# Two stacked attention layers on one core: the last 128-row TensorE products rewritten as pairs of 64-row products, with a new order table

## The chip, the cores and the metric

The kernel runs on one NeuronCore of a Trainium2 chip. The metric is the device time of one execution in microseconds (us), from start to end; lower is better. A core has TensorE (PE, matrix products into PSUM), VectorE (DVE), ScalarE (ACT), GpSimd (POOL) and SyncE (SP, which here issues DMAs and nothing else). Each engine works through its own queue in order; semaphores tie the queues together. PSUM has 128 partitions and eight banks of 512 f32 values each.

## The reference, cut to what matters

The input x is 2048 tokens of 512 bf16 values. Two layers of A and B follow each other, each with a layer norm in front and a residual behind, 32 heads of 16 dimensions:

```python
x = x + A(layernorm(x)); x = x + B(layernorm(x))     # twice
# A: 4 segments of 512 tokens; causal softmax attention within a segment,
#    mixed by a gate per head with a linear-attention memory of earlier segments
a_dot = softmax(q @ k.T * scale + mask) @ v
a_mem = (phi(q) @ M) / (phi(q) @ z + 1e-6)            # M, z summed over earlier segments
o = g * a_mem + (1 - g) * a_dot;  return o @ wo
# B: linear attention over all tokens with a learned feature map per head
phi_q = concat(softmax(q @ w_phi), softmax(-(q @ w_phi)))     # phi_k alike
o = (phi_q @ (phi_k.T @ v)) / (phi_q @ sum(phi_k) + 1e-6);  return o @ wo
```

## The kernel before, in words

Sixteen token tiles of 128 rows stay in SBUF as X. The program first describes the whole computation as a list of 2729 operations (class Graph), each with its reads and writes, the engines that could do it and a modelled duration. The order of the work is not computed in the kernel: a packed table, ORDER (L1181), holds for every operation its place in one global order and its engine, and for every tile its buffer. `place` (L157) unpacks it, and `emit` (L190) gives each engine its operations in that order with the semaphore waits that the dependencies need. Tile pools are small: PSUM is pool pD, four tiles of two banks each, so a product can only start when an earlier tile's copy out of PSUM is done.

The helpers matter for reading the profile, because a line there is the helper's:

- `mm` (products at L326) and `pair` (products at L341). Nearly all products contract over 64 rows: the lower and the upper half of the array work on two products at the same time, which write two different banks. `pair` makes one projection out of two operations: in the first, the halves of the array work on one half of the contraction of each of two outputs, in the second they swap. The second waits for the first (`hard`). In the table they are separate operations (labels such as KQ and KQ2), so other work can stand between them.
- `evac` (ScalarE copy at L359, VectorE copy at L360): a copy out of PSUM, on the engine that the table names. ScalarE also does all exponentials (`act`, L351).
- `tpe` (L371, products at L378): transposes a 128 x 512 block as four 128-row, 128-column products against the identity, into bf16 values in one bank, followed by one `evac`. It is used for the blocks listed in PE_T (L1171): the first four normalised tiles of layer 0 and of layer 1 (xnT, xA), tile 15 of the second norm in each layer (xnT, xB), one attention output in each layer (otr), and the four transposed key features of the first segment (PhKtr). All other transposes are DMA transposes (L364).
- `fold_weights` (L548): multiplies the transposed B query and key weights by the block-diagonal w_phi, eight operations of four 128-row, 128-column products each (label fold, seen at L326), each with an `evac` into WB.
- `o_T` (L885, products at L894): for six tiles of B's output (blocks ("b", ...) in PE_T) the sum of the two halves and the transpose are done at once, with eight 128-row, 128-column products, two accumulated into each of four column blocks of one bank (label otp), followed by an `evac` (ote).
- `setup` (L450) loads, makes constants and computes the gates from one small product (label beta); `warm` (L652) issues 26 products of 512 columns over 128 rows at the start, with some smaller ones in the middle, whose result nobody uses.

Per layer, `build` (L1106) goes over four segments: norm, projections (`a_proj`), attention for two tiles at a time (`a_att`), output projection, second norm, B's keys (`b_keys`); then over four chunks of B's queries (`b_query`), with the next layer's norm and projections behind each chunk. In the span, the first layer's attention lies roughly from 10 to 185 us, its B queries from 207 to 232, the second layer's attention from there to 400, and its B queries from 427 to the end.

Of the kernel before, what the change touches and what calls it, by code (L numbers as in the profile page):

```python
# [12 lines left out]
BF16 = mybir.dt.bfloat16  # L13
# [284 lines left out]
class Kernel:  # L298
# [72 lines left out]
    def tpe(self, out_ap, src, reads, writes, opens=(), label="", ev=None):  # L371

        ps = self.T(self.pD, "gen")
        pb = lambda: ps.t[:, :].bitcast(BF16)[:, 0:512]

        def fn(e):
            for k in range(4):
                ins = e.transpose(pb()[:, k * 128:(k + 1) * 128], src()[:, k * 128:(k + 1) * 128], self.ident[:])  # L378
# [71 lines left out]
    def setup(self):  # L450
# [74 lines left out]
        self.mm(lambda: [(pb.t[:, 0:H], self.onesb[:], self.beta_sb[:], True, True)], [H], [R("beta0"), R("onesb")], [pb], label="beta")  # L525
# [22 lines left out]
    def fold_weights(self):  # L548
# [12 lines left out]
        for k in ("k", "q"):  # L561
# [90 lines left out]
    def warm(self):  # L652
# [232 lines left out]
    def o_T(self, key, o, ores, pair=None):  # L885
        R = self.R
        oT = self.oT[key] = self.T(self.p1, "oT")
        if pair is not None:
            tp = self.T(self.pD, "gen")

            def fn(e):
                for k in range(4):
                    for sgn in range(2):
                        ins = e.matmul(tp.t[:, k * 128:(k + 1) * 128], pair.t[:, (k // 2) * 512 + sgn * 256 + (k % 2) * 128:(k // 2) * 512 + sgn * 256 + (k % 2) * 128 + 128],  # L894
                                       self.ident[:], start=sgn == 0, stop=sgn == 1)
# [290 lines left out]
6=sjk_%$N<cBVm5bf)gMs4uYRyBILp0m=8PR2pkL>Aun!%UtlHt3I%X8`~(HD6TXHx*cAt3TpWtsa0m{=__zcU;8L6e_wg;Q0^;cq52wLuNQjwWCd`F?)SpITYwUre
unl&`HP9Wq;94k*MQ|Q0!=Eq@FwTcJ@Dsg-p7;%{z;9s;F2~}y74G2A)C*T)MI4PqaW{;`arllhLkWz)N>~ib;sh**kr;(p;2ms%iC7X#VR@{8Ww0`?!zwrfOJh~6h
HG#=&cwB-a0))a=lC=Jg4MAG{)z&(!3$i48mHoFG?)nYLI5Pj{ZI(U<1y$%ed#zHftvUk&cQ<v1CK%=9)^eb3&lc*ckv#6hY}y5X2YN31o{Fe;aseR6KOJzq1spnU*
k*s0Fe*|vEVU|rCB%|=ixM*j~lQ!jic$f5C_l#EJ5RGASI_sG?`M+_xJ<G#JU(8>!HOjF&G=;SD2CtQxVES2OuY9rEHXo4nl6qPMRz;zo#Y`fP(9z;|ACef2F4Qftq
0s`bf=j1sSrGhgMPqe2wp+5w^f6$V+dq2L<6<+(h{(1bb2_zQc{Uj2vyI<+KTrHe*RDMFprR?ZaY}pO(;4+K)+S5EZ0CREA1ZQaXTx=@5ov818}{7{FU_CrS>aZ}0<  # L1190
_rE)ZchEfu&OG&XFeT!Rh7w*Pnv<J&meQH1{Fd1$`qG6O0dr@N=PO0!U9Y&xXz_b$%;(H9BCRCY5(<tgqRj4-Ap^;RTYEm^CK^18cHKayViKb8uszudlF*T)T)SMLW
#qF4iDiClB5_ALu`3<F}sdNgb(R7+cGw3wVq`0((&fr=)hw*4G&896hhrXe8^bvz7Ic|seG>_&}OIlB>Xf=IFt!O-dMHBcK_T}T)kAvx3+Dai5N=GpvoyXSHhEC!M{
ET+c7qo%4(bu$#cG7m*NSClb58%s~hxgKG{+#yEZpzDJIEqr^S&X0y7)~)Lj4t98yo&p1KeeS!6iKPMCy(Vc+>3)a7YFk=PC&UiEgzr|K1i`)0mY<H?o12mG!)@TF2
qH-Fh_AQF3vZxH{ZfO9D~F7HkRg6oP%?60se|h@-_ULhw^nS!J9cB=jVbvjKet*C8itLj@nZf>OiNUBXy;2REA?wS&mI7Au})LEu4jy@IX$-gLxvS=RrJ#NAOf0$-{
XPPvfkdjbm~w&cNBZ9CxR<kdfoS2`JB!GI1PIbcnv-FZnRl;v*EnN2xZ?=IK0&XYge1&Q*90PvNTEgDY`mp2hWeA<yI_T%Q;5M&86p`52w1*gThy(+N65XK5avq+~p
w&(V2`!^^n>U!)aWksEMBuEUq8E?4IoT#XxZBd*DpDLG$&xZH%Bax+fJ7onPn$5*Mk*v>mRJ}2O<oPoA+MyevxP$o*mX{oA6M_1??rKjt3gPQXNTEM618{Wgac_lC9
Z+R6j;}*P@*KtcOBwBH6Zo?fp1s4{(cr|a}oxFxW@_NoEKIbChGX{}g6csn=J%8X^q=gZCxh=Qj_S}j0@qX^iUAQaXq1%+0t+-20NTI|%`i_D{ka)|NK!^arB2c{JA
1E^=<jatX4{$f`z!d}u6bHGN2oa&8qUbFuiOS*-e@}<`2%qAk{4*C5zi@F;O1$P;qO|yxYl{n9N7NM;`4Ye3AE|&SBhJ8CXdudphN6ZjD6Vi#@sLW0M^sYu6aB?$KE
r4E7$4{R^nfn&ISvz#=?T>r%|v-oPeh4wqPd76Vv1Pe1x1KR@sdt(BhgsAqN^NVBoI$2v4|()ir6BdNFtJoXVgk06LCZ$@tm%4Ymr=}5G_PXkxHZ%H~Ad&5$EAN$Ao
ZklGBJ=JV;#Umf{BY6@$ePF;v{<JA9YhiT2_icMu&#9x+mk5M4xC@g4ubc|{ZPJ+~3*L|c(wWE0s%29ZPL6uCr3@grvvnMD>+MRpQZWe?F=^c3AhS1~|z7ms+L7%qm  # L1200
1$9z?c5~IZ!F;-NQ_xT||;OcUmXex4xtl}v@;cH^Nm?0*J>*9uZ#xuopo+u`XSz@x7BBqMjVvblOR*S{rCBNWlVy>7c=8FYlp;#i8iC4T!>=tW84Y^b-7eDcIu}AC^
8^wCDNvsen#VWB`Y!IJ`FT{SaPOKH5i!a63;w!O5d?RYgL!yQ{EG~+gs+K$=YRm27Td_lI6_><8u~!@r$HY;wQydp3#5QqKoDpZm8F@~e78k@RabDC?m&FxPTip@2#
Vv7D+!go4cj9~TgZNR@k<Y~oaaNv__r-bnKs*xlWL;TbHjqu^W6@AvkQe1^aY;6k55-IIN<0xy#ZRKKY$~6LX7Y`=EUTyw;;OtNugUAOyKF8$iWah}>LYu|x1z7SA@
9haMN0{?r|czBz7zfAd(mJ1B7T%NWi>^zy1FIrOP1|r2l=bGErX<zccqpc<vkfJg_P1rD??<cjFfR@n2eIW<p5bv)mL>?UDZlHmOse`>O0w5elHuUC-P@GP=?DvGKP
#P+sJq_zDyt^q>}+Mmi$4+mI-Ai8Am3PiDjT{rQXOSvXL4rTdTLSze*}I$|5qE9H3ImOfs{4D%;8jvWc1?8>@-(nS3bU$)+lmOevGg6!N{CCYz~WWKr2!wv$~X>8=v
=blFW7ldMq}myx=JjMB~3QMFfPk&omD`CLwtljRIKQyx=O<gYTVEGhS?{i?mnDi5d*DqO#iyH$jKDTSUYU(3?6lpG~z$suyI94hyy7E0=Da*P}+hsoh`oXjb6$r19E
Y^id{f-+Qx=|Zxw?5MKK*>a>DFHfpds=N9qd#Il3v^t}Xs}l+os^t2JI;hU6v&!j1>aa?yQ|JJ_QhrdYWIFv(<(8dPFLhqEQ5RGmnMSUbb7X#9Kr200Y8_ASm#Osu8
# [70 lines left out]
```

## Time and profile before

| what | value |
|---|---|
| time, median of three runs | 469.15 us (468.43, 469.15, 469.81) |
| span of the profiled execution | 465.9 us |
| time of the profiled execution itself | not shown; the median is 3.25 us over the span |
| mean granted TensorE clock | 0.999 |

The span runs from the first to the last instruction. In the page and in the answers of the trace, a group row gives line, engine, operation, tiles, shapes and count, then the busy time in us and the mean of one in ns, then the idle time of the engine just before the group. A row of the chain gives start, length, engine, tile, line and count, following back from the last instruction whatever released each step. A row of the timeline gives start, length, engine, line and count; a length over several instructions runs from the first start to the last end, and a product's length includes the time that its result takes to come out, so products overlap and their starts tell the pace. PEld is the weight load that belongs to each product. A row of the waits gives who waited for whom, us in total, times and the longest.

### The profile page before, as it was taken

The numbers are of one execution on the slowest core, as the hardware profiler recorded it, in microseconds if no ns is written. First come the engines' busy times: TensorE is split into PE (matmuls) and PEld (weight loads), VectorE is DVE, ScalarE is ACT, GpSimd is POOL, SyncE is SP. The second block draws the span as 40 slices with busy tenths as digits, with TensorE's granted clock in tenths as the row PEclk, the third lists the DMA queues.
The fourth block names the chain that finished last, engine by engine and source line by source line (L and its number), as shares of the span: only waits on it lengthen the run. The fifth ranks groups of instructions, "written<-read, shape, count | busy, mean of one in ns | idle before, by whom it ended". The sixth has DMA issues, their size and how long they took to land.

```text
span 465.9 us, 25071 instructions
## 1 busy us (share of the span) xinstructions
PE 448.2 (96%) x11591; PEld 296.7 (64%) x11591; DVE 418.9 (90%) x801; ACT 424.3 (91%) x550; POOL 53.3 (11%) x139
## 2 busy tenths in 40 slices
PE   9999999999999999999999999999999999999886
PEld 4467656767767676655556777676677677666553
DVE  6999999999879988988999999999999787998991
ACT  4899999999999998589999999999999999686984
POOL 1401131001101101100320041010020020110000
PEclk9999999999999999999999999999999999999999
DMA  8363673403743031000143443441206104100247
GB/s 258 80 150 77 94 147 65 75 13 53 95 83 50 4 56 37 14 3 14 31 87 61 72 82 61 73 87 33 25 16 106 26 16 61 38 13 3 48 82 216
DMA packets 89386, 30.34 MB, mean 65 GB/s; under 512 B 75954, under 2 KB 89282, under 8 KB 89282
## 3 DMA queue, kind: packets, MB, share of 16 engines
q1 hardware_dynamic: 88450, 28.20, 32.5%
q8 instruction: 91, 1.49, 1.3%
q10 hardware_dynamic: 800, 0.52, 0.4%
q14 instruction: 13, 0.11, 0.1%
q0 software_dynamic: 32, 0.02, 0.0%
HBM read 6.31 MB, written 2.10 MB: 18 GB/s over the span
## 4 chain that ended last, share of the span: by engine, by line
PE 67%; ACT 26%; DVE 4%; issue 2%; POOL 1%; DVEq 0%
PE D L341 42%; PE D L326 23%; ACT p L351 12%; ACT pF L351 8%; ACT pE L351 4%; PE D L662 2%; DVE p L1091 1%; ACT pS L351 1%; PE D L378 1%; DVE p L360 1%; ACT X L359 1%; POOL rstd L590 1%; ACT p L359 0%; DVE p L601 0%; DVE p L1097 0%
## 5 line engine op out<-in xcount | busy, mean ns | idle before, releaser
L351 ACT ACTIVATE p<-D 128x1024 bf16<-128x1024 f32 (+1 forms) x224 | 222.0, 1026 | 13.2 <-PE D L341 10.0
L351 ACT ACTIVATE pF<-D 128x896 bf16<-128x896 f32 x128 | 116.1, 934 | 3.1 <-PE D L326 2.2
L326 PE MATMUL D<-pK,pQ 64*128 64x256 bf16 (+3 forms) x1536 | 114.8, 243 | 4.2 <-ACT pF L351 1.0
L326 PEld LDWEIGHTS D<-pK,pQ 64*128 64x128 bf16 x1536 | 55.1, 94 | 40.8 <-ACT pF L351 6.5
L326 PE MATMUL D<-pV,pF 64*128 64x34 bf16 x1024 | 76.4, 176 | 0.5 <-ACT pE L351 0.5
L326 PE MATMUL D<-pW,pF 64*128 64x34 bf16 x1024 | 74.1, 176 | 0.0
L326 PEld LDWEIGHTS D<-pV,pF 64*128 64x128 bf16 x1024 | 56.7, 93 | 3.7 <-issue 0.8
L588 POOL TENSOR_SCALAR rstd<-mv 128x1 f32<-128x1 f32 x60 | 15.2, 259 | 352.9 <-DVE mv L581 352.9
L326 PE MATMUL D<-pV,p 64*128 64x34 bf16 x1024 | 53.4, 176 | 0.6 <-issue 0.4
L326 PEld LDWEIGHTS D<-pW,pF 64*128 64x128 bf16 x1024 | 53.4, 93 | 1.0
L351 ACT ACTIVATE pE<-D 128x768 bf16<-128x768 f32 x64 | 52.4, 828 | 1.3 <-PE D L326 1.0
L326 PE MATMUL D<-pW,p 64*128 64x34 bf16 x1024 | 52.4, 176 | 0.0
L326 PEld LDWEIGHTS D<-pV,p 64*128 64x128 bf16 x1024 | 47.5, 93 | 3.2 <-issue 0.5
L326 PEld LDWEIGHTS D<-pW,p 64*128 64x128 bf16 x1024 | 46.0, 93 | 1.6
L326 PE MATMUL D<-tri,two 64*128 64x128 bf16 (+1 forms) x384 | 46.1, 234 | 0.0
L326 PE MATMUL D<-pV,pE 64*128 64x34 bf16 x512 | 45.1, 175 | 0.0
L580 DVE BATCH_NORM_STATS2 stats<-X 128x6 f32<-128x512 bf16 x64 | 42.7, 682 | 1.9 <-DMA X<-in_A_x_dram 1.5
L326 PE MATMUL D<-pW,pE 64*128 64x34 bf16 x512 | 43.4, 175 | 0.0
L972 DVE TENSOR_REDUCE pS<-p 128x64 f32<-128x1024 bf16 (+1 forms) x36 | 38.8, 1089 | 1.4 <-ACT p L351 1.4
L341 PE MATMUL D<-pX,WA_q 64*128 64x512 bf16 x256 | 37.1, 377 | 0.1
L341 PE MATMUL D<-pX,WA_k 64*128 64x512 bf16 x256 | 36.9, 377 | 0.1
L590 POOL TENSOR_TENSOR rstd<-rstd,mhalf 128x1 f32<-128x1 f32 x60 | 35.1, 599 | 3.1
(130 smaller groups left out, 986.2 us busy)
## 6 DMA issues: line engine op xcount, KB each, us to landing
pW<-pV SPq DMA_DIRECT2D x16, 136.0 KB, 3.1
out_dram<-X SPq DMA_DIRECT2D x7, 256.0 KB, 3.2
X<-in_A_x_dram SPq DMA_DIRECT2D x3, 512.0 KB, 5.6
pX<-in_B_wqkv_dram SPq DMA_DIRECT2D x3, 512.0 KB, 4.7
p<-p SPq DMA_TRANSPOSE x76, 3.0
pX<-p SPq DMA_TRANSPOSE x54, 3.3
WA_k<-in_A_wk_dram SPq DMA_DIRECT2D x2, 256.0 KB, 6.7
WB_o<-in_B_wo_dram SPq DMA_DIRECT2D x8, 64.0 KB, 3.0
```

The lines of the kernel that those rows point to most:

```text
L326: ins = e.matmul(out_ap, lhsT, rhs, start=st, stop=sp, tile_position=(basep(lhsT), basep(out_ap)))
L341: ins = e.matmul(out_ap, lhsT[64 * hf:64 * hf + 64], rhs[64 * hf:64 * hf + 64], start=k == 0 and i == 0, stop=k == 1 and i == len(lists[hf ...
L351: return self.g.op({"act": (dur, lambda e: e.activation(out_ap(), in_ap(), func, scale=scale))}, reads, writes, opens, label=label)
L359: ch = {"act": (n / 1.2 + 51, lambda e: e.activation(out_ap(), in_ap(), ACT.Copy)), "dve": ((340 if fast else n / 0.96 + 65), lambda e: e. ...
L360: "dve": ((340 if fast else n / 0.96 + 65), lambda e: e.tensor_copy(out_ap(), in_ap()))}
L378: ins = e.transpose(pb()[:, k * 128:(k + 1) * 128], src()[:, k * 128:(k + 1) * 128], self.ident[:])
L580: v(lambda e: e.bn_stats(self.stats[:, t, :], self.X[:, t, :]), 602, [R("X", t)], [R("st", t)], label="bn")
L588: v(lambda e: e.tensor_scalar(rs, self.mv[:, t, 1:2], LN_EPS, None, op0=ALU.add), 170, [R("mv", t)], [R("rstd", t)], eng="pool", label="rstd")
L590: v(lambda e: e.tensor_tensor(rs, rs, self.mhalf[:], ALU.pow), 540, [R("rstd", t), R("mhalf")], [R("rstd", t)], eng="pool", label="rstd")
L662: ins = e.matmul(D.t[c0:, r0 * 8:r0 * 8 + n], r[:, c0:], ones(r, n), start=True, stop=True, tile_position=(r0, c0))
L972: fn = lambda e, sgn=sgn, eo=eo, Z=Z, n=n: e.tensor_reduce(Z.t[:, 0:64 * n].rearrange("p (k s h) -> p k s h", k=n, s=2)[:, :, sgn, :], eo( ...
L1091: v(lambda e, Ns=Ns, Tm=Tm, w=w, shape=shape: e.tensor_tensor(shape(Tm.t[:]), shape(Ns.t[:]), w(), ALU.mult), 600, [Ns, AB[0], AB[1]], [Tm ...
```

## The change

Every product that used 128 rows now uses 64: a transpose, a fold and an output transpose are split over the two halves of the array, and the two halves write two different banks, each 64 columns of every block (the small gate product uses the lower half alone). So a transpose has eight products with 64 moving columns in place of four with 128, an output transpose sixteen in place of eight, and the copies out of PSUM read f32 from two banks, with the halves put side by side again by the access pattern. The transposes are ordinary products now (result f32) where they were `transpose` instructions with a bf16 result. A warm-up unit becomes two concurrent 64-row products, and the one group of small 128-row products in it is left out, so there is one operation fewer. The order table is replaced as a whole.

```diff
--- before.py
+++ after.py
@@ -371,17 +371,20 @@
     def tpe(self, out_ap, src, reads, writes, opens=(), label="", ev=None):
 
         ps = self.T(self.pD, "gen")
-        pb = lambda: ps.t[:, :].bitcast(BF16)[:, 0:512]
 
         def fn(e):
             for k in range(4):
-                ins = e.transpose(pb()[:, k * 128:(k + 1) * 128], src()[:, k * 128:(k + 1) * 128], self.ident[:])
+                for hf in range(2):
+                    r = slice(64 * hf, 64 * hf + 64)
+                    ins = e.matmul(ps.t[:, hf * 512 + k * 64:hf * 512 + k * 64 + 64], src()[r, k * 128:(k + 1) * 128], self.ident[r, r], start=True, stop=True,
+                                   tile_position=(64 * hf, 0))
             return ins
-        self.g.op({"pe": (240.0, fn)}, list(reads) + [self.R("ident")], [ps], opens=opens, label=label + "p")
+        self.g.op({"pe": (112.0, fn)}, list(reads) + [self.R("ident")], [ps], opens=opens, label=label + "p", rows=64)
+        halves = lambda: ps.t[:].rearrange("p (h x) -> p h x", h=2)[:, :, 0:256].rearrange("p h (a c) -> p h a c", a=4)
         if ev:
-            self.evac(ev[0], lambda: ev[1](pb()), 512, [ps], writes, label=label + "e")
+            self.evac(ev[0], lambda: ev[1](halves()), 512, [ps], writes, label=label + "e")
         else:
-            self.evac(out_ap, lambda: pb().rearrange("p (a b) -> p a b", a=4), 512, [ps], writes, label=label + "e", fast=True)
+            self.evac(lambda: out_ap().rearrange("p a (h c) -> p h a c", h=2), halves, 512, [ps], writes, label=label + "e")
 
     def recip(self, e, o, i):
 
@@ -522,7 +525,7 @@
         v(lambda e: e.memset(self.eps6[:], 1e-6), 70, [], [R("eps6")])
         gt = self.gt
         pb = self.T(self.pD, "gen")
-        self.mm(lambda: [(pb.t[:, 0:H], self.onesb[:], self.beta_sb[:], True, True)], [H], [R("beta0"), R("onesb")], [pb], label="beta")
+        self.mm(lambda: [(pb.t[:, 0:H], self.onesb[0:64, :], self.beta_sb[0:64, :], True, True)], [H], [R("beta0"), R("onesb")], [pb], label="beta", rows=64)
         self.act(lambda: gt[:, 0, :], lambda: pb.t[:, 0:H], ACT.Exp, 32, [pb], [R("gt")])
         v(lambda e: e.tensor_scalar(gt[:, 1, :], gt[:, 0, :], 2.0 ** 60, 1.0, op0=ALU.min, op1=ALU.add), 100, [R("gt")], [R("gt1")])
         v(lambda e: e.reciprocal(gt[:, 2, :], gt[:, 1, :]), 270, [R("gt1")], [R("gt2")])
@@ -568,10 +571,11 @@
                 self.tr(lambda W=W, dt=dt: W.t[:, :, dt * 128:(dt + 1) * 128], lambda raw=raw, dt=dt: raw.t[:, dt, :], [raw], [W[dt]], label="foldT")
             for dt in range(4):
                 ps = self.T(self.pD, "gen")
-                self.mm(lambda ps=ps, dt=dt, W=W: [(ps.t[:, g * 128:(g + 1) * 128], W.t[:, g, dt * 128:(dt + 1) * 128],
-                                                    Wbd.t[:, g * 128:(g + 1) * 128], True, True) for g in range(NG)],
-                        [128] * 4, [W[dt], Wbd], [ps], label="fold")
-                self.evac(lambda k=k, dt=dt: self.WB[k][:, dt, :], lambda ps=ps: ps.t[:, 0:512], 512, [ps], [R("WB", k, dt)], label="folde")
+                self.mm(lambda ps=ps, dt=dt, W=W: [(ps.t[:, hf * 512 + g * 64:hf * 512 + g * 64 + 64], W.t[64 * hf:64 * hf + 64, g, dt * 128:(dt + 1) * 128],
+                                                    Wbd.t[64 * hf:64 * hf + 64, g * 128 + hf * 64:g * 128 + hf * 64 + 64], True, True) for g in range(NG) for hf in range(2)],
+                        [], [W[dt], Wbd], [ps], label="fold", rows=64, dur=112.0)
+                self.evac(lambda k=k, dt=dt: self.WB[k][:, dt, :].rearrange("p (g h c) -> p h g c", g=NG, h=2),
+                          lambda ps=ps: ps.t[:].rearrange("p (h x) -> p h x", h=2)[:, :, 0:256].rearrange("p h (g c) -> p h g c", g=NG), 512, [ps], [R("WB", k, dt)], label="folde")
 
 
     def ln(self, t, xT, flex=False, pe=False, root="pool"):
@@ -663,9 +667,9 @@
                 return ins
             self.g.op({"pe": (m * max(n / 2.4 + 2.5, 26.0), fn)}, [self.R("onesb")], [D], label="warm", rows=rows if c0 == 0 else rows * 10)
         for k in range(N_WARM):
-            unit(128, 512, 1)
+            unit(64, 512, 1)
             if k == N_WARM // 2:
-                for rows, n, m in ((64, 51, 12), (64, 64, 8), (64, 256, 4), (128, 34, 8)):
+                for rows, n, m in ((64, 51, 12), (64, 64, 8), (64, 256, 4)):
                     unit(rows, n, m)
 
     def a_proj(self, L, s):
@@ -891,11 +895,15 @@
             def fn(e):
                 for k in range(4):
                     for sgn in range(2):
-                        ins = e.matmul(tp.t[:, k * 128:(k + 1) * 128], pair.t[:, (k // 2) * 512 + sgn * 256 + (k % 2) * 128:(k // 2) * 512 + sgn * 256 + (k % 2) * 128 + 128],
-                                       self.ident[:], start=sgn == 0, stop=sgn == 1)
+                        for hf in range(2):
+                            r = slice(64 * hf, 64 * hf + 64)
+                            c0 = (k // 2) * 512 + sgn * 256 + (k % 2) * 128
+                            ins = e.matmul(tp.t[:, hf * 512 + k * 64:hf * 512 + k * 64 + 64], pair.t[r, c0:c0 + 128], self.ident[r, r], start=sgn == 0, stop=sgn == 1,
+                                           tile_position=(64 * hf, 0))
                 return ins
-            self.g.op({"pe": (440.0, fn)}, [pair, R("ident")], [tp], opens=[oT], label="otp")
-            self.evac(lambda: oT.t[:], lambda: tp.t[:, 0:512], 512, [tp], [oT], label="ote")
+            self.g.op({"pe": (220.0, fn)}, [pair, R("ident")], [tp], opens=[oT], label="otp", rows=64)
+            self.evac(lambda: oT.t[:].rearrange("p (a h c) -> p h a c", a=4, h=2),
+                      lambda: tp.t[:].rearrange("p (h x) -> p h x", h=2)[:, :, 0:256].rearrange("p h (a c) -> p h a c", a=4), 512, [tp], [oT], label="ote")
         elif key in PE_T:
             self.tpe(lambda: oT.t[:].rearrange("p (a b) -> p a b", a=4), lambda: o.t, ores, [oT], [oT], label="otr")
         else:
@@ -1179,64 +1187,62 @@ ORDER = """
...
```

Unpacked against the list of operations, the two tables hold the same operations but for the warm-up group. The new one places them in another order and changes the engine of some copies: of the ten copies behind xnT transposes 6 are on ScalarE (4 before), of the six behind output transposes 2 (3 before), of the eight behind folds 1 (0 before), of the four weight permutations 1 (0 before), of 36 evacuated residuals 7 (9 before), of 18 query copies 5 (4 before); two of five memsets go from GpSimd to VectorE.

More of the change, by code (lines that the diff above doesn't have):

```diff
@@ L1186 @@
[L1186 to L1197, printed above, removed]
@@ new lines @@
+2T!OCf6AXjgFdTA1cbEtxAQ{|-QE(Z0z(@#z0r(?igI<sedSMP&0C!+C42GW}JKlwb&>M4N7!1VT&=Vd&9|(uF5Cl2!A$$&5AvLCjT(}OdKzh6ei{Lt>!BEJ6tKcc##(vNSf
+5zpo9#+FMTna6)EiQq3Fcu!cBp3tzuqCd6zOW1y!(_Mt{c%3@hqQPHr@(Vu0V^RLK86AC1++uph1edygeUL|^ued_0kYsYScH8sGiJpHI1@7A3&@7~a2V#rj0pG=hT}lUgLg
+4E4uV<m8e${jc*u_vU^W!M=g<M;;46rW9dQFZ#EtL_24Ni71YPhGm;v!{Fa|(D9D<9nE5^sZv=ipQP+WpjLGg6xM+tBTj7Gvy_yR{@CwxY&a3n^;r_dQcgQeIS=fZMahTX9n
+PJ?++2!F&kv;r&OE@145J@6|ij1_SV7DLTr@oOl88KF3q!ADpW!|@tk$3S?A-#}>`kN2=FmcX}E63gKPjKECrIX*^#Z(tjg!tyvBtKxI2f~&AHRzl?a7>S=^HLQ*+aRy4v44
@@ new lines @@
+LOnisE_wc;cTx$}o}eQI(FX_&@yv#C(8pJq=bb^#805zy(zE5Ii?#5hjNw2s06ZR93MTdd^r8%+NcLq>AzJ^zgarhLutznIE1m)fAPfFN^;V-eLiiq8c}gkB14OX29IU-GTO
+Tq8ZIoxxcv9iSfl*A6Mv(>+T^xbN3&8UkeF=+{QHsHMK6w6Ui%PKs?J>rA9P!-u_WF#4d1MOlWyqJbfN*kQUIfxtP;5bP6tk2bi6O#s$OB0jUu1sQy=;K=mjXr;9Q>UEJgWR
+!;_QnIJ*zUn<9(o4NWR?o^5rS95a>G?`X~`0!+cmlu)k-a&m#-Lzy9Q6iOTv?;Q43*1qr{i{^Oso_Pl8yu|z<Wx7qIq`||D8HtApt^Q9IIN1w{PY6<dq9)i)e%@I)=L&<r7`
+xxwP3-@$~kv~;FB6>zdlrJha5#T4b#}Vh}H~4M)SQHHY=-Fq(8%qy#5r*1JxTF9d2)^2kf^Z+Rd<^#QRn}vF07W+kPauReMnI^qdwQ-2wyXk#FHKQ`{Uz&BEfk`=4@X1I!9J
+)snmqmhy#)JE^(f7jqS=oj6o3xGqk9!#SWu+5Ad&s`>Fo^kG=;O~XdNHl4HW2e(&rBQa0{30^);U@3RYe`BFtM1@My2V8h|kCY2gs(%QOd}^ynxfh{6nqT90O4CcI+tV2L2F
@@ L1240 @@
+a)=BBaIj>hAzV|S^_q_r6eWDxIS_<Zs4zr$t%jY(VB=*h+#}L|0g(KOR{
 """
```

92 lines of the change are left out of this document (46 added, 46 removed).

## Prediction

> **What bounds the kernel now.** I read the busy shares first, then the chain of waits, then a table of stretches.
>
> ```profile
> span 465.9 us, 25071 instructions
> PE 448.2 (96%) x11591; PEld 296.7 (64%) x11591; DVE 418.9 (90%) x801; ACT 424.3 (91%) x550; POOL 53.3 (11%) x139
> PE 67%; ACT 26%; DVE 4%; issue 2%; POOL 1%; DVEq 0%
> ```
>
> Three engines are over 90% busy. The chain runs through TensorE (PE) for 67% and through ScalarE (ACT) for 26%, so a shorter PE pays in some stages and not in others. The stretches tell which:
>
> ```profile
> 30.00:60.00 30.00, 28.88 (x918) 20.65 (x919) 28.66 (x69) 29.81 (x36) 5.31 (x13) 1.00 0.59 100
> 120.00:150.00 30.00, 29.31 (x848) 19.83 (x846) 26.71 (x48) 29.37 (x36) 3.24 (x8) 1.00 0.52 75
> 180.00:212.00 32.00, 31.01 (x692) 19.82 (x690) 27.97 (x54) 23.36 (x36) 3.14 (x8) 1.00 0.07 15
> 212.00:240.00 28.00, 27.11 (x548) 15.53 (x546) 26.91 (x66) 27.50 (x40) 5.54 (x12) 1.00 0.18 36
> 390.00:413.00 23.00, 22.94 (x489) 14.43 (x486) 19.25 (x29) 17.82 (x26) 3.25 (x8) 1.00 0.24 43
> ```
>
> The columns are length, then busy time of PE, weight loads, VectorE (DVE), ACT and GpSimd, then clock, DMA share and GB/s. In 30 to 60 ACT is idle for 0.2 us of 30: a shorter PE alone brings little there. In 180 to 212 and 390 to 413 ACT has 8.6 and 5.2 us to spare, and PE alone sets the end. In 212 to 240 all three are close to full. The granted clock is 1.00 throughout, so no clock effect is counted.
>
> The profiled execution's span is 465.9; the median of the three times is 469.15, which leaves 3.25 us around the span if that execution was a median one. Only the span is shown for it. I work on the span and add 3.25.
>
> **TensorE: what a 128-row product costs.** Nearly all products use 64 rows, two at a time. The exceptions are these forms:
>
> ```profile
> L378 PE MATMUL D<-ident,p 128*128 128x128 bf16 x64 | 6.1, 221 | 0.5 <-DVE p L601 0.5
> L894 PE MATMUL D<-ident,p 128*128 128x128 bf16 x48 | 3.6, 220 | 0.2 <-DVE p L1091 0.2
> L326 PE MATMUL D<-p,pX 128*128 128x128 bf16 x32 | 3.2, 221 | 0.4 <-ACT pF L351 0.4
> ```
>
> That is 64/4 = 16 transposes, 48/8 = 6 output transposes and 32/4 = 8 folds. Four transposes lie in the warm-up, which is 128-row itself. One visit, in order of time on PE, and one output transpose:
>
> ```profile
> 184.65 0.59 PE L341 MATMUL D<-pX,WB_q 64*128 64x512 bf16 x4
> 185.17 0.40 PE L378 MATMUL D<-ident,p 128*128 128x128 bf16 x4
> 185.50 0.82 PE L341 MATMUL D<-pX,WB_q 64*128 64x512 bf16 x6
> ...
> 438.20 0.59 PE L341 MATMUL D<-pX,WB_q 64*128 64x512 bf16 x4
> 438.73 0.62 PE L894 MATMUL D<-ident,p 128*128 128x128 bf16 x8
> 439.32 0.39 PE L341 MATMUL D<-X,ident 64*128 64x512 bf16 x2
> ```
>
> A pair of 64-row products of 512 columns starts every 0.216 us (1.73 us for 16 in the chain row quoted further on), so the next start was due at 184.65 + 2 x 0.216 = 185.08. The transpose starts at 185.17 and the next product at 185.50: the visit costs 0.42. Four products of 128 columns start over (0.40 - 0.221)/3 = 0.06 apart, 0.24 in all, so about 0.18 is the change to 128 rows and back. The output transpose was due at 438.63 and its follower starts at 439.32: 0.69.
>
> The trace has no transpose in 64 rows, but it has the same shape, 64 moving columns with a weight load for each product:
>
> ```profile
> 212.37 0.40 PE L326 MATMUL D<-Rkv,p 64*128 64x64 bf16 x16
> L326 PE MATMUL D<-Rkv,p 64*128 64x64 bf16 x512 | 12.3, 189 | 2.3 <-ACT p L351 2.1
> L326 PEld LDWEIGHTS D<-Rkv,p 64*128 64x128 bf16 x512 | 10.3, 93 | 7.4 <-ACT p L351 4.0 <-DVE p L360 0.4
> ```
>
> Eight pairs start (0.40 - 0.189)/7 = 0.03 apart. A transpose or fold becomes four pairs, 0.12; an output transpose eight pairs, 0.24. **Saved: 0.30 a visit, 0.45 an output transpose.** Outside the warm-up that is 12 x 0.30 + 8 x 0.30 + 6 x 0.45, less about 0.4 where visits share their switches: some 8.3 us of PE. One visit is bounded by 0.30 saved and 0.32 lost (eight loads of 93 ns in a row are 0.74).
>
> [...] The trace does not bear the serial reading out: 16 such loads of 93 ns lie beside 16 products that took 0.40 in all.
>
> **What of this is on the path.** The chain around the visits:
>
> ```profile
> 183.51 1.73 PE D L341 x16
> 185.24 0.33 PE D L378 x4
> ...
> 192.31 0.40 PE D L378 x4
> ...
> 402.58 0.33 PE D L378 x4
> ...
> 412.54 0.33 PE D L378 x4
> ```
>
> *PE alone.* These four transposes are on the chain where nothing else is near: 4 x 0.30 = -1.2.
>
> ```profile
> 51.36 2.87 PE D L326 x114
> ...
> 131.69 1.23 PE D L326 x76
> ...
> 158.07 1.93 PE D L326 x109
> ...
> 170.82 0.65 PE D L326 x8
> ```
>
> *Folds.* These pieces hold five of the eight folds (51.36 holds two), 1.5 us. ACT is almost full beside them (0.2 and 0.6 us idle in the rows above), so ACT is late next. I take half, -0.75; bounds 0 and -2.4.
>
> *Query stages.* The chain has
>
> ```profile
> 212.83 0.63 PE D L894 x8
> ...
> 229.00 0.40 PE D L378 x4
> ...
> 455.19 0.62 PE D L894 x8
> ```
>
> The first and last output transposes pay, 2 x 0.45, and one transpose 0.2: -1.1. The other transposes at 226 to 228 stand behind DVE and POOL and pay nothing, and neither do the four in 29 to 40, where the chain is on ACT.
>
> *Start.* The chain begins with warm-up products.
>
> ```profile
> 1.11 7.52 PE D L662 x77
> ```
>
> Halved into two concurrent products, a warm-up unit lasts as long as before. Unpacked, the new table puts 20 full and 3 short units ahead of the first transpose, where the old has 21 and 4, and two of the last ones between the halves of the first projections. The first transpose was waiting for this queue, so the projections can begin about 0.35 earlier; the ScalarE copies of 0.6 each are late next. I take -0.3; bounds 0 and -0.4.
>
> **What is added: dearer evacuations.**
>
> ```profile
> L360 DVE COPY pX<-D 128x512 bf16<-128x512 bf16 x6 | 2.4, 414 | 1.4 <-PE D L378 1.4
> L360 DVE CAST WB_q<-D 128x512 bf16<-128x512 f32 x4 | 2.8, 688 | 0.0
> L360 DVE CAST pK<-D 128x1024 bf16<-128x1024 f32 x13 | 15.9, 1220 | 2.7 <-PE D L341 2.6
> L359 ACT ACTIVATE pX<-D 128x512 bf16<-128x512 bf16 x4 | 2.2, 597 | 0.8 <-PE D L378 0.8
> ```
>
> A transpose's result is now f32 in two banks: 0.69 on DVE instead of 0.41, still 0.60 on ACT. The new table has 8 of them on DVE (10 before) and two more on ACT: 8 x 0.69 - 10 x 0.41 = +1.4 us of DVE, +1.2 of ACT. It also moves one fold copy and one weight permutation (half-size copies, some 0.7 on DVE, 0.6 on ACT) to ACT; one output-transpose copy and two half-size residual copies the other way; one full query copy (1.22 on DVE) to ACT; two short memsets from POOL to DVE. In sum DVE gains 1.4 - 1.4 + 2.1 - 1.2 + 0.3 = 1.2 us and ACT 1.2 + 1.2 - 1.8 + 1.2 = 1.8. Most of it lies beside PE. The four copies of transposed keys, 4 x 0.28 = 1.1, fall between 29 and 41 us, where DVE has 1.3 of 30 us free. I take +0.6; bounds 0 and +3.0.
>
> **The order.** Of 1054 PE operations 678 keep their relative order (the longest common run); a PE operation moves 2 places on average, 18 at most, an ACT operation 3, a DVE operation 6.5. So this is the old schedule shuffled locally. SP's queue is shuffled too: some of its loads and DMA transposes move by 10 to 70 places, but the table of waits has no DMA among its long waits except for the first block of x. One structural count can be priced. Every projection is two halves, and the second waits for the first to finish:
>
> ```profile
> 11.39 0.82 PE L341 MATMUL D<-pX,WA_q 64*128 64x512 bf16 x2
> 11.83 0.39 PE L341 MATMUL D<-pX,WA_k 64*128 64x512 bf16 x1
> ...
> PEld D L341 <- PE D L341: 5.2, 13, 0.6
> ```
>
> The fourth pair starts at 11.39, the next at 11.83 instead of 11.61: 0.22 lost where nothing stands between the halves. The table of waits counts 13 such waits, and the old table has 13 adjacent halves; the new has 9. Four fewer are worth 0.9, about the chain's PE share of it: -0.5. The rest of the shuffle has no row; I put it at 0 and bound it by the evacuation term's +3.0 one way and the unpaid PE time the other.
>
> **Sum:** -0.3 - 1.2 - 0.75 - 1.1 - 0.5 + 0.6 = -3.25 us. Span 462.65, time 465.9.
>
> **Rivals.**
> *All of PE's saving passes* (the new order also rebalances ACT): -8.3 - 0.9 - 0.3 = -9.5, or 459.7. For it: the chain is two thirds PE. Against: ACT's 0.2 us of idle time in 30 to 60, with a PE that has 1.1. Chance 0.07.
>
> *Hidden anyway:* only the PE-alone stretches pay (-1.2), the start 0.3, and the copies take their +0.6 back: -0.9, or 468.3. For it: full ACT and DVE in every other stretch quoted. Chance 0.17.
>
> *The evacuating engines become the bound, slower:* the added 1.2 us of DVE and 1.8 us of ACT are all paid, in 30 to 60 and 212 to 240, where both have at most 1.3 us free, and PE then waits for banks; its shorter work only becomes longer idle time: +3.0, or 472.2. It decides from the point where the copies' paid time exceeds PE's paid saving by 1.4 us. For it: three full engines and a reshuffled order of which the trace shows nothing. Against: the stretches in which PE is alone pay in any case. Chance 0.19. [...] The rows 0.41 against 0.69 agree that the copy gets no cheaper.
>
> *The 64-row visits bring nothing* (their weight loads run one after another): ten transposes and folds on the chain cost 0.32 more each, the two output transposes 16 x 0.093 - 0.69 = 0.8 more each: +4.8, with the other terms +4.6, or 473.8. Against it the Rkv rows. Chance 0.03.
>
> **Numbers.** The forecast has 0.54: 465.9, its own range 462 to 467.7. A measurement of this kernel tells about 0.3% (1.4 us) from no change. Faster than 467.7: 0.54 + 0.07, and a little of the hidden case, 0.63. Within 0.3%: the rest of it, 0.15. Slower: 0.22. The range 461.5 to 472.2 leaves out most of the first rival and the last, and the worst of the third.
>
> **What would show it.** Right: no 128-row form in the groups; a transpose visit of about 0.12 between its neighbours; weight-load idle behind a first half in about 9 cases; the stages 180 to 212 and 390 to 413 shorter by 0.6 us or more each; copies of 0.69 on DVE. Wrong: visits still 0.3 or more apart; ACT or DVE busy over 29.8 of 30 us with PE idle longer than before; a start no earlier than 10.7 us; a stage without any 64-row visit that became longer by 1 us or more, which would be the order.

## The result, and the profile after

The changed kernel takes **473.0 us** (median of four runs, 472.4 to 474.0) where the kernel before takes 468.8 beside it: 1.0086 times as long, interval 1.0065 to 1.0106, about 4 us slower. The profiled execution took 472.73 with a span of 471.0, so 1.7 us lie around it. The forecast was 465.9 with a range of 461.5 to 472.2.

The page of the changed kernel, busy shares and then the chain:

```profile
span 471.0 us, 25402 instructions
PE 446.6 (95%) x11753; PEld 299.1 (64%) x11753; DVE 421.5 (90%) x801; ACT 423.8 (90%) x552; POOL 57.4 (12%) x137
PE 61%; ACT 27%; DVE 6%; DMA 3%; issue 2%; SPq 1%; POOL 0%; DVEq 0%
```

TensorE (PE) is busy for 1.6 us less, not for 8 us less, and two entries are new in the chain: DMA with 3% and SP's queue with 1%. The five stretches of the prediction, in its columns:

```profile
30.00:60.00 30.00, 27.39 (x912) 19.87 (x912) 27.80 (x65) 28.40 (x35) 3.17 (x4) 1.00 0.44 68
120.00:150.00 30.00, 28.24 (x840) 20.24 (x835) 25.76 (x47) 28.63 (x34) 3.65 (x8) 1.00 0.41 61
180.00:212.00 32.00, 31.31 (x715) 20.24 (x713) 29.07 (x55) 22.78 (x34) 3.23 (x8) 1.00 0.10 22
212.00:240.00 28.00, 26.27 (x592) 15.01 (x590) 27.01 (x62) 28.00 (x43) 6.41 (x12) 1.00 0.16 31
390.00:413.00 23.00, 22.83 (x604) 15.99 (x598) 19.29 (x32) 18.56 (x28) 2.22 (x6) 1.00 0.27 44
```

In 30 to 60 and 120 to 150 TensorE now idles 2.6 and 1.8 us (1.1 and 0.7 before), and ACT idles longer too: neither was the bound there, so something else held both. The waits name it only in part; first a row of before from the table of waits, then the rows of after:

```profile
PEld D L341 <- issue: 5.5, 16, 1.0
```

```profile
PEld D L341 <- issue: 10.8, 27, 1.6
PEld D L341 <- PE D L341: 4.6, 11, 0.6
PE D L326 <- issue: 2.2, 4, 1.1
PE D L341 <- DMA p<-p: 1.5, 2, 0.9
```

"Issue" is idle time that no semaphore ends, as far as the trace shows. The new copies have the forms foreseen, 0.69 us on DVE:

```profile
L360 DVE CAST pX<-D 128x512 bf16<-128x512 f32 x4 | 2.7, 687 | 0.5 <-PE D L379 0.5
L379 PE MATMUL D<-ident,p 64*128 64x64 bf16 x128 | 4.5, 191 | 1.0 <-ACT p L351 0.5 <-DVE p L605 0.2
```

**Where the time went.** Matching the same operation in both traces gives how much later it starts in after. The shift is -0.5 us at 20 to 30, 0.0 to +0.5 at 40 to 125, +2.2 at 180, back to +1.0 at 230 (here the expected gain shows), +1.6 at 250 to 310, then +3.3 at 320, 3.4 to 4.0 until 450, and 4.5 at the end. The largest step is one wait:

```profile
316.93 0.22 PE L326 MATMUL D<-tri,two 64*128 64x128 bf16 x2
318.53 0.39 PE L341 MATMUL D<-WB_k,pX 64*128 64x512 bf16 x2 [1.38 <-issue]
```

The timeline calls it issue, but the product's input is a DMA transpose (xnT1882, by the numbers of before's list of operations) that landed at 318.44. SP's part of the timeline shows why it was late:

```profile
308.70 0.60 SPq L740 DMA_DIRECT2D pW<-pV  x1
309.34 8.48 SPq L364 DMA_TRANSPOSE pX<-p  x5
```

Five transposes stand in one row, issued 1.3 to 2.1 us apart. xnT1882 was ready at 309.25 and issued at 314.12, behind xnT1674, which nobody needs before 328.8. In before it was issued at 310.30, ahead of xnT1674. No product of 310 to 320 us was rewritten: this is the prediction's own sign for the order, a stage without any 64-row visit that became longer by 1 us or more.

### The profile page after: what moved, and what is told of

It is laid out like the page before. It is cut to its first block, busy times and chain, and to the rows that moved or that the text cites. A ratio compares the mean times of both kernels' runs of the same rounds, so it can differ in the third digit from the quotient of the medians.

```text
span 471.0 us, 25402 instructions
## 1 busy us (share of the span) xinstructions
PE 446.6 (95%) x11753; PEld 299.1 (64%) x11753; DVE 421.5 (90%) x801; ACT 423.8 (90%) x552; POOL 57.4 (12%) x137
## 4 chain that ended last, share of the span: by engine, by line
PE 61%; ACT 27%; DVE 6%; DMA 3%; issue 2%; SPq 1%; POOL 0%; DVEq 0%
PE D L341 38%; PE D L326 21%; ACT p L351 15%; ACT pF L351 6%; ACT pE L351 3%; DMA p<-p 2%; PE D L666 2%; DVE X L933 1%; DVE stats L584 1%; ACT pS L351 1%; DMA pX<-p 1%; SPq L364 1%; ACT p L359 1%; ACT X L359 1%; DVE p L878 0%
## 5 line engine op out<-in xcount | busy, mean ns | idle before, releaser
L592 POOL TENSOR_SCALAR rstd<-mv 128x1 f32<-128x1 f32 x60 | 19.8, 341 | 347.8 <-DVE mv L585 347.5
L341 PE MATMUL D<-WB_k,pX 64*128 64x512 bf16 (+1 forms) x288 | 33.8, 353 | 2.2 <-issue 1.4
```

What stands on the lines that cost most here:

```text
L341: ins = e.matmul(out_ap, lhsT[64 * hf:64 * hf + 64], rhs[64 * hf:64 * hf + 64], start=k == 0 and i == 0, stop=k == 1 and i == len(lists[hf ...
L592: v(lambda e: e.tensor_scalar(rs, self.mv[:, t, 1:2], LN_EPS, None, op0=ALU.add), 170, [R("mv", t)], [R("rstd", t)], eng="pool", label="rstd")
```

## The experiments

The table gives, for each run, its ratio to the kernel before on the same chip, and from its profiled execution the span, TensorE's busy time, and its gaps between products of over 0.1 us by what ended them. "Blocks" are gaps without a semaphore whose next product starts 1.2 to 1.6 us after a packet of instructions has landed (explained below). "DMA, other" holds the waits for a DMA and the rest without a semaphore, such as the 1.38 above. DVE leaves out the 1.1 us in which the first product of every kernel waits for a constant.

| kernel | ratio, interval | span | PE busy | ACT | DVE | blocks | DMA, other |
|---|---|---|---|---|---|---|---|
| before | 1 | 465.9 | 448.2 | 8.1 | 1.9 | 1.0 | 0.3 |
| after | 1.0086, 1.0065 to 1.0106 | 471.0 | 446.6 | 8.3 | 3.3 | 2.4 | 3.6 |
| e1, new order alone | 1.0090, 1.0069 to 1.0112 | 472.4 | 450.7 | 7.6 | 3.5 | 1.8 | 3.1 |
| e2, 64-row products alone | 1.0198, 1.0173 to 1.0223 | 477.3 | 447.6 | 9.4 | 5.9 | 7.5 | 0 |
| e3, after, SP by due time | 1.0028, 1.0011 to 1.0045 | 468.4 | 444.9 | 8.5 | 4.3 | 1.6 | 2.0 |
| e4, before, blocks moved | 1.0238, 1.0214 to 1.0262 | 478.3 | 451.1 | 8.1 | 2.9 | 9.9 | 0.2 |
| e5, after, blocks moved | 1.0075, 1.0050 to 1.0101 | 468.0 | 444.3 | 7.8 | 3.9 | 1.2 | 4.1 |
| e6, e3 and blocks moved | 1.0005, 0.9989 to 1.0021 | 467.9 | 444.2 | 7.8 | 3.9 | 1.9 | 3.2 |
| e7, e2 and blocks moved | 1.0140, 1.0113 to 1.0166 | 476.0 | 448.4 | 9.6 | 5.7 | 5.9 | 0 |
| e8, four late visits | 0.9979, 0.9964 to 0.9994 | 465.1 | 447.3 | 8.5 | 1.9 | 0.8 | 0.3 |
| e9, transposes alone | 1.0064, 1.0048 to 1.0080 | 469.7 | 449.6 | 7.8 | 3.8 | 1.4 | 0.3 |

From before to after the columns give -1.6 (busy), +0.2, +1.4, +1.4 and +3.3: 4.7 of the 5.1 us by which the span grew.

### The two halves of the change (e1, e2) and SP's queue (e3)

The first two take the change apart: the new table with the old 128-row products, and the 64-row products with the old table. The third leaves after as it is and exchanges neighbours in SP's queue (25 exchanges, 34 of 187 entries) where the later one is needed first and is ready.

```diff
 e1: before.py with the ORDER of after.py
-                for rows, n, m in ((64, 51, 12), (64, 64, 8), (64, 256, 4), (128, 34, 8)):
+                for rows, n, m in ((64, 51, 12), (64, 64, 8), (64, 256, 4)):
 e2: after.py with the ORDER of before.py
-                for rows, n, m in ((64, 51, 12), (64, 64, 8), (64, 256, 4)):
+                for rows, n, m in ((64, 51, 12), (64, 64, 8), (64, 256, 4), (64, 34, 8)):
 e3: after.py, SP's entries in ORDER, for example near 309 us
-... vsw, xnT1686, xnT1876, xnT1674, xnT1882, xnT1680 ...
+... xnT1686, vsw, xnT1876, xnT1882, xnT1674, xnT1680 ...
```

> The new order table with the old 128-row products (the group of small warm-up products left out, so that the table fits). Two theories of the 4 us loss. Order: the 64-row products save about 2.8 us at a fixed order, as the prediction had it without its term for adjacent halves, and the new order costs about 7; then this kernel takes 475 to 477 us. Products: the new order is worth nothing either way, and the copies from two banks cost the 4 us; then it takes 468 to 470.

> The 64-row products with the old order table, so every operation in its old place on its old engine (the small warm-up group kept, in 64 rows). Theory order: 465 to 467 us. Theory products: 472 to 474.

> The changed kernel with nothing moved except in the DMA queue: of the DMA transposes and small copies, one that is ready and needed earlier goes ahead of one needed later (25 exchanges of neighbours, loads untouched). Theory DMA queue: the late transposes that TensorE waits for in the changed kernel (1.4 us in one place, some 4 in all, against 1.8 before) are what the order costs, so this gives back 2 to 3 us: 470 to 471. Rival, the order on TensorE and the copying engines costs it: within 1 us of the changed kernel, 472 to 474.

Measured 474.3, 479.3 and 471.25 us, with 469.9 for the kernel before. **Both halves alone are slower than before, and the products by twice as much as the order**, so neither theory stands as it was stated. The two losses, 0.9 and 2.0%, do not add up to the 0.9% of both together either; each half has its own place for the blocks described below. e3 bears out the DMA queue: its interval lies below that of after, and 0.0058 of the ratio, 2.7 us, is given back, though 471.25 is a little over the 470 to 471 expected. TensorE has the same order of products in both. Matched one by one, the profiled execution of e3 gains 1.55 us at the wait near 317, which is gone. It gains another 0.8 between 434 and 440, and that is not the queue's: there the granted clock of after's execution fell to 0.50 for 3.4 us, and that of e3 did not. (Two executions of after at a clock of 1.00 took 473.28 and 474.02, so this fall is not its loss.)

The surprise is e2, in whose row no DMA wait stands, but 7.5 us of gaps that no semaphore ends, inside operations:

```profile
44.57 0.18 PE L326 MATMUL D<-pV,pF 64*128 64x34 bf16 x1
46.18 0.19 PE L326 MATMUL D<-pW,pF 64*128 64x34 bf16 x2 [1.43 <-issue]
```

These two are products of one operation; nothing lies between them but the next instruction. The page of before has this row in its list of DMA queues:

```profile
q8 instruction: 91, 1.49, 1.3%
```

91 packets of 16,384 bytes stand beside TensorE's program of 2 x 11591 products and weight loads, and the burst of the last experiment (e10), with 2 x 1024 of them more than after, has 100 packets where after has 92. That is 64 bytes an instruction, so a packet holds 256 of them, a block of some 127 products with their weight loads. In the packets' records the one ahead of this gap ran from 43.53 to 44.75, and 1.42 us later the products went on. The gaps of e2 stand at the 728th, 856th, 1364th, 1872nd, 2383rd product: multiples of some 127 apart. It is the number that counts and not the product: nine of the eleven kernels of the table have a gap without a semaphore at product 1872, which is seven different products of the work in them. A new theory follows: a block cannot begin before its packet is in, and the packet is not asked for before the block ahead has begun. Dense streams of 34-column products use a block up faster than the packets follow each other, 3.2 us apart at the least (the one ahead of a gap at 149.04 in e2 in 2.1 us) and then wait.

### Moving the blocks (e4 to e7)

To count what a table costs by this theory, I took the product starts of a trace, left the gaps out, set a border every 127.2 products and held each block until 3.4 us after the start of the one before (an estimate: the ten closest packets of before start 3.2 to 3.5 us apart). It gives 1.9 us for before, 5.1 for after, 11.4 for e2. Moved by 16 products, before has 6.5 to 7.5, and by 41 it has 10; after has its least, 1.1, at 12. Removing a few small warm-up products moves every border and leaves all other work as it is.

```diff
 e4: before.py
-                for rows, n, m in ((64, 51, 12), (64, 64, 8), (64, 256, 4), (128, 34, 8)):
+                for rows, n, m in ((64, 51, 1), (64, 64, 1), (64, 512, 5), (128, 34, 1)):
 e5: after.py, and e6: the kernel of e3
-                for rows, n, m in ((64, 51, 12), (64, 64, 8), (64, 256, 4)):
+                for rows, n, m in ((64, 51, 6), (64, 64, 8), (64, 256, 4)):
 e7: the kernel of e2
-                for rows, n, m in ((64, 51, 12), (64, 64, 8), (64, 256, 4), (64, 34, 8)):
+                for rows, n, m in ((64, 51, 1), (64, 64, 5), (64, 512, 4), (64, 34, 8)):
```

> The kernel before with nothing changed but its warm-up groups: 41 small products fewer ((64,51,12), (64,64,8), (64,256,4), (128,34,8) become (64,51,1), (64,64,1), (64,512,5), (128,34,1)), about the same time in them (43 ns apart by the paces of the rows), same order table, same products behind. TensorE's instruction stream is brought in by 16,384-byte packets (91 of them, 127.2 products each), so every border between two packets' worth of instructions moves by 41 products. Fetch theory (a block of instructions cannot begin before its packet, asked for when the block before it began, is in, some 3.4 us): counted on the trace of before, the blocks as they lie would be held 1.9 us in all and the moved ones 10.1; the stalls without a semaphore (1.3 us in gaps over 100 ns) grow to 5 to 9 us, and the time to 473 to 478 from the 469 to 470 of the kernel before. Rival (the stalls are made by DMA traffic or by copies, and where the blocks lie is nothing): within 1.4 us of the kernel before.

> The changed kernel with six pairs of small warm-up products fewer ((64,51,12) becomes (64,51,6)), nothing else: each border of the instruction blocks moves by 12 products. Fetch theory: counted on the trace of the changed kernel, holding falls from 5.1 to 1.1 us (2.8 us of it were seen as gaps), so 469.5 to 471.5 instead of 473.0, stalls without a semaphore under 2 us. Rival: 472.5 to 473.5, the stalls where they were in time.

> The changed kernel with SP's queue in the order in which its transfers are due (the third experiment, 471.25) and the same six pairs of warm-up products fewer. Fetch theory and DMA-queue theory together: the two gains add, 467.5 to 470. Rival: 471 to 471.6.

> The 64-row products in the old order (the second experiment, 479.33) with 28 small warm-up products fewer, about the same time in them ((64,51,12), (64,64,8), (64,256,4) become (64,51,1), (64,64,5), (64,512,4)). Fetch theory: counted on that run's trace, holding falls from 11.4 to 5.7 us, so 473 to 477, and the stalls of 1.43 at 44.75, 1.44 at 63.45 and 1.19 at 85.76 are gone or smaller. Rival (dearer copies and banks that come free late): 478.5 to 480.

**e4 settles that the place of the borders counts: 480.4 us, 11 us slower than before, with no other work changed than 41 small warm-up products.** The same products in the two timelines, before and then e4:

```profile
42.41 0.27 PE L326 MATMUL D<-tri,two 64*128 64x256 bf16 x2
42.52 0.18 PE L326 MATMUL D<-pV,p 64*128 64x34 bf16 x1
```

```profile
42.50 0.27 PE L326 MATMUL D<-tri,two 64*128 64x256 bf16 x2
44.21 0.19 PE L326 MATMUL D<-pV,p 64*128 64x34 bf16 x1 [1.44 <-issue]
...
62.88 0.19 PE L326 MATMUL D<-pW,pF 64*128 64x34 bf16 x2 [1.81 <-issue]
```

Up to 40 us every operation starts within 0.1 us of its time in before. Then the shift climbs in steps that stand at the gaps, +1.6 at 43, +2.9 at 61, and later stages give back some 0.3 us of a step at most; it ends at 12.5. The stalls, 10.1 us, and the time exceed the 5 to 9 us and the 473 to 478 expected. Part of the loss is in busy time (451.1 against 448.2), which may be holds too short to open a gap, though no run shows it; 0.4 of it comes at 448 us, where the granted clock of this execution fell to 0.50 for 3.4 us. Counted on e4's own trace, the least holding lies 40 products back, where before has its borders.

e7 gains on e2 by the same means, 2.7 us by the ratios and 3.7 between the medians (475.6, as expected), but of the three gaps named two are gone and the third has only moved with its border (1.21 us at 83.9). e6 takes 469.85, 1.4 us less than e3 (1.1 by the ratios, whose intervals overlap) and **not to be told from before**: the two edits together take back nearly all of the loss. How much of e6's gain is the blocks' is not settled: its block gaps are no fewer than e3's, and its profiled execution begins the first projection at 9.96 instead of 10.72, most of which is another cause (last section). e5 missed: its median is 473.2, no better than after, though its profiled execution is its fastest run (469.8) and has half the block gaps. Its runs spread from 469.8 to 476.2. In that trace the waits for DMA are larger, 4.1 us against 3.6, with SP's order as in after. So for the changed kernel itself the gain from moving the blocks is not shown. Its runs go with the granted clock in part: the four at 0.999 or 1.000 have a middle value of 471.2, within the range expected, the eight at 0.991 to 0.996 one of 473.4. Why they spread so far beyond that stays open.

### The parts of the products that pay, and that cost (e8, e9)

e8 changes only visits that move no border ahead of 402 us; e9 changes only the transposes, the part with dearer copies.

```diff
 e8: before.py; tpe64 and the second branch are the code of after.py
     def tpe(self, out_ap, src, reads, writes, opens=(), label="", ev=None):
+        self.nt = getattr(self, "nt", 0) + 1
+        if self.nt > 14:
+            return self.tpe64(out_ap, src, reads, writes, opens, label)
...
+            self.no = getattr(self, "no", 0) + 1
+            if self.no > 4:
 e9: before.py with the tpe of after.py
-                for rows, n, m in ((64, 51, 12), (64, 64, 8), (64, 256, 4), (128, 34, 8)):
+                for rows, n, m in ((64, 51, 1), (64, 64, 3), (64, 512, 4), (128, 34, 8)):
```

> The kernel before with its own order table, in which only the last four 128-row visits of the second layer (the attention output's transpose near 402 us, one transpose of a normalised tile near 412, the output transposes near 438 and 455) use 64 rows; they come so late that no block border ahead of 402 us moves (counted on the trace of before, holding is 2.2 us against 1.8). Theory (64-row visits pay what the prediction said where TensorE is alone, and only the moved blocks, the dearer copies and the new order cost): 2 x 0.30 + 2 x 0.45 = 1.5 us at most, 0.8 by the start-to-start times of the second experiment; 467.9 to 468.7 where the kernel before takes 469.4. Rival (a 64-row visit saves the end nothing even there): within 0.4 us of the kernel before.

> The kernel before with its own order table, in which only the sixteen transposes use 64 rows (folds and output transposes stay in 128), with 32 small warm-up products fewer in about the same time, which is where the blocks lie best for it (counted on the trace of before: 4.8 us of holding against 1.8). Copies theory (f32 copies of 0.69 instead of 0.41 us on DVE make the banks come free late; the products-only kernel had 4.0 us more of waits for DVE): fetch +2.3, waits for DVE +3 to +4, products -2.4, so 472 to 474 where the kernel before takes 469.4. Fetch-only theory (the copies are hidden): 469 to 470.5.

**e8 takes 468.74 us against 469.62: faster than both kernels**, by 0.2% (0.06 to 0.36, so the rival's 0.4 us is not excluded by the times alone). Its timeline at the first transpose and the two output transposes:

```profile
401.45 1.03 PE L341 MATMUL D<-pX,WB_q 64*128 64x512 bf16 x8
402.39 0.29 PE L397 MATMUL D<-ident,p 64*128 64x64 bf16 x8
402.51 1.03 PE L341 MATMUL D<-WB_v,pX 64*128 64x512 bf16 x8
...
438.19 0.40 PE L920 MATMUL D<-ident,p 64*128 64x64 bf16 x16
438.88 0.39 PE L341 MATMUL D<-X,ident 64*128 64x512 bf16 x2 [0.29 <-ACT p L351]
...
454.74 0.41 PE L920 MATMUL D<-ident,p 64*128 64x64 bf16 x16 [0.16 <-DVE p L1129]
454.98 0.38 PE L341 MATMUL D<-X,ident 64*128 64x512 bf16 x2
```

The next product follows 0.12 us after the first visit begins and 0.24 after the last, as forecast. From the product ahead to the product behind, the first visit takes 1.06 us where before took 1.29 (401.56 to 402.85): 0.23 saved. The transpose near 412, whose next product follows after 0.24 and not 0.12, saves 0.19, the output transpose near 455 saves 0.32, and the one near 438 nothing, because its follower now waits 0.29 for an exponential on ACT. Together 0.74, half of the 1.5 that the prediction's prices give. Operations ahead of the first visit start earlier too in this execution, by 0.6 up to 385 us and by 0.1 at 401; that part is not the edit's.

e9 takes 472.4. That is the number of the copies theory, but not all of its reason: in the profiled execution 0.86 us is a later start that has nothing to do with copies (last section), and the waits for DVE grew by 1.9, not by 3 to 4. What the copies do is seen at the second layer's first projections, which wait for the transposed tiles:

```profile
230.69 0.29 PE L379 MATMUL D<-ident,p 64*128 64x64 bf16 x8 [0.78 <-DVE p L604]
230.81 0.41 PE L326 MATMUL D<-Rkv,p 64*128 64x64 bf16 x16
231.62 0.41 PE L326 MATMUL D<-Rkv,p 64*128 64x64 bf16 x16 [0.40 <-DVE pX L360]
232.22 0.39 PE L341 MATMUL D<-pX,WA_k 64*128 64x512 bf16 x2 [0.19 <-DVE pX L360]
```

TensorE finishes the transposes at once and waits 0.6 us for the copies, which take 0.69 each; in before two of 0.41 were done at 229.95 and the projection began at 230.00.

### The supply of instructions by itself (e10)

```diff
 e10: after.py
-                for rows, n, m in ((64, 51, 12), (64, 64, 8), (64, 256, 4)):
+                for rows, n, m in ((64, 51, 12), (64, 34, 520), (64, 256, 4)):
```

> The changed kernel with 512 more pairs of 64-row products of 34 columns in the warm-up ((64,64,8) becomes (64,34,520)), that is 1024 products or eight blocks of instructions in a row with nothing to wait for. Fetch theory: TensorE takes in a block of 127 products no faster than one in some 3.4 us, so eight blocks take 26 to 29 us, with a halt at each border of a block. Rival (fetch is hidden; the array sets the pace): 0.03 us a pair as in the rows of the kernel before, 15 to 16 us, without halts.

One run, 505.2 us, 32 more than after. Its timeline in the burst:

```profile
8.33 1.17 PE L666 MATMUL D<-onesb 64*128 64x34 bf16 x80
12.84 1.90 PE L666 MATMUL D<-onesb 64*128 64x34 bf16 x128 [3.35 <-issue]
17.94 2.00 PE L666 MATMUL D<-onesb 64*128 64x34 bf16 x128 [3.19 <-issue]
21.67 2.00 PE L666 MATMUL D<-onesb 64*128 64x34 bf16 x128 [1.73 <-issue]
25.67 2.00 PE L666 MATMUL D<-onesb 64*128 64x34 bf16 x128 [2.00 <-issue]
29.68 2.00 PE L666 MATMUL D<-onesb 64*128 64x34 bf16 x128 [2.00 <-issue]
```

**Runs of exactly 128 products, 256 instructions, and a halt after each.** From start to start a block takes 3.5 to 4.0 us (the two behind the last row begin at 33.13 and 36.86) although its work takes 2.0, with almost no other transfer under way (the row of the stretch: DMA share 0.02). Next to the start's loads it takes 5.1. All 1040 products of the burst take 31 us (7.2 to 38.3), above the 26 to 29 of the theory for 1024 and twice the 15 to 16 of its rival. Each halt ends 1.2 to 1.5 us after a packet's end. In the packets' records the next packet starts 1.1 us after the first product of each block from 17.94 on and lasts 1.1 to 1.4, so it indeed starts only after the block ahead has begun; when it is asked for, the records do not show. The first halt comes after 223 products.

```profile
20.00:25.00 5.00, 2.00 (x128) 1.89 (x128) 0.00 (x0) 0.00 (x0) 0.00 (x0) 0.50 0.02 3
```

The same row has a granted clock of 0.50, which lasts from 13.5 to 40.9 us. The halts do not need it: the first one ended at 12.84, and all of e4's lie outside the fall of its clock at 448, so at 1.00, and the 128 products take 1.90 us in the block that begins at 1.00 and 2.00 in the others. What a block of the burst would take at 1.00 throughout, no run shows.

The fetch is not hidden here, against the rival: 9.9 us of e4's gaps stand at borders, and the burst is held for about half its time (15.5 of 31 us by the waits). The longest run of its products without a halt is the first, of 223.

## Why the prediction was wrong, point by point

- **64-row visits are cheap** (0.12 and 0.24): right but for a seam. **Their saving, 0.30 and 0.45, was too large**: e8 has 0.19 to 0.23 and 0.32. The prediction counted the change to 128 rows and back, about 0.18, as gone; a new visit still begins about 0.07 after the product was due (402.39 for 402.31 in e8). TensorE's busy time fell by 1.6 in after, whose clock fell for 3.4 us, and by 4.0 at most (e6), not by 8.3.
- **PE alone, -1.2; query stages, -1.1**: the shift between the traces falls by 1.2 between 180 and 230 and by 0.3 around 400. The mechanism is right; the size is two thirds of the forecast here, where the order changed too, and half in e8 (0.74 of 1.5).
- **Folds, -0.75**: not seen; between 45 and 175 us the shift grows by more than 1.4.
- **Start, -0.3**: the first projection is at 10.52 instead of 10.73. Starts differ by more than that for another reason (below), so this is no evidence.
- **Copies, +0.6, bounds 0 and +3.0**: waits for DVE grew by 1.4 in after and by 4.0 with the old order (e2); the new table may hide part of them.
- **Adjacent halves, 13 to 9, -0.5**: the waits count 11, with 4.6 us against 5.2.
- **"The rest of the shuffle has no row; I put it at 0"**: this is the step that failed, and with it the argument that SP's moves have no price because no DMA is among the long waits of before. What its table left was slack: counted from landing to first product, one of 137 DMA transposes of before was used within 0.1 us of its landing, and seven in after. Putting SP's queue nearer to the order of need gave back 2.7 us (e3), with five such transposes left. A queue without waits had nothing to give back in before and something to lose.
- **Left out of the sum altogether: the blocks of instructions.** The 162 added products (11753 against 11591) and the new order move all borders. After has 1.4 us more of visible gaps at them, the old order with the new products 6.5 more. The "issue" rows of before stood in its table of waits, and the prediction gives them no term. SP's order and six pairs of warm-up products fewer together bring the changed kernel back to 1.0005 of before; of that, only SP's part has an interval of its own.
- **The 3.25 us added for the time around the span** were too many: 1.7 lie around it in the changed kernel, and 2.1 to 2.3 in the later runs of before. The span itself was forecast at 462.65 and measured at 471.0.
- The rival with the evacuating engines as the bound came out at 472.2, near the measured time, but for another reason: ACT's waits are unchanged, and DVE's are 1.4 of the loss. That the copy gets no cheaper is borne out by 0.687 us in after against 0.414 in before.

## What to carry to other kernels

Count instructions as a resource with a rate: here TensorE got 256 of them in 3.5 us at best in the burst, and no two packets of its program start less than 3.2 us apart in any of the runs. So the dense stream of short products in e10 was bound by its supply (3.5 to 4.0 us a block for 2.0 us of work), and splitting products in two brought 6.5 us more of gaps at borders in e2, with 0.6 us less of busy TensorE. Idle time without a semaphore, at product numbers that are a fixed step apart (some 127 here), was the sign; 41 products fewer at the start showed it, and in this tuned program they alone cost 2.4% (e4). A queue in which the trace shows no wait may owe that to the slack that its order leaves (one of 137 DMA transposes used within 0.1 us of its landing in before, seven in after): before reordering it, list for each transfer when it is ready, issued, landed and first used.

## What the runs showed of the hardware that was not expected

- A product behind a border starts 1.2 to 1.6 us after its packet ends (74 gaps of the eleven kernels, middle value 1.41). The band is the one by which these gaps were picked, but all except one of 0.11 us also stand within six products of a border, by number. At product 3149 three kernels have a gap of 0.3 us that ends later, 1.8 to 2.2 after the packet.
- The warm-up products run 0.43 us apart at first and 0.215 later, and the moment of the change differs between executions. Before and then e9, with busy TensorE products counted by the microsecond:

```profile
4.00:5.00 1.00, 1.00 (x6) 0.46 (x5) 0.77 (x2) 0.00 (x0) 0.00 (x0) 1.00 1.02 332
```

```profile
4.00:5.00 1.00, 1.00 (x4) 0.38 (x3) 0.68 (x2) 0.00 (x0) 0.00 (x0) 1.00 1.02 337
5.00:6.00 1.00, 1.00 (x5) 0.42 (x4) 1.00 (x4) 0.28 (x1) 0.00 (x0) 1.00 1.02 324
```

It is 4.06 us in before and in e6, 4.90 in after, 5.69 in e9. The clock column says 1.00 throughout, but each trace's first record of the granted clock begins only at about that moment (4.04, 4.04, 4.87 and 5.58 us), and the column has nothing to show for the time ahead of it. The first transpose moves with it by up to 0.9 us.
- Short falls of the granted clock (3.4 us at 0.50 in the traces of after and e4) come and go between executions of one kernel: e7 took 474.65 to 474.86 us at a mean clock of 0.999 or 1.000 and 476.3 to 478.1 at 0.993 to 0.996. They are more frequent in some kernels: the mean clock is under 0.998 in 43 of the 63 runs of after and e1 to e7, and in 3 of the 40 of before beside e1 to e7. In e8 and e9 the runs with such falls are not slower as a group: 467.35, 467.56 and 469.24 us for a median of 468.74 in e8, 471.87 and 473.29 for 472.44 in e9. What the falls add to the loss was not tested.
